# One pass of Strassen products with a second level in five of seven, operands kept in DRAM

## The chip, the cores and the metric

The kernel runs on one core of one Trainium2 chip. The metric is the time of one execution in device microseconds (us), the median of several. A profiled execution is about 1.7 us shorter, because its span runs only from the first to the last instruction. A verdict is a ratio: the mean time of one kernel's fast runs over that of the other's of the same rounds, with a 95% interval; it is called "same" where the two lie within 2%, so a "same" can still be a small difference clear of noise. So it is not quite the ratio of the medians quoted. Engine names: PE is TensorE, DVE is VectorE, ACT is ScalarE, POOL is GpSimd, SP issues DMA.

## The reference, cut to what matters

A linear attention block, then a gated MLP, each behind a layer norm and with a residual. Only the MLP matters here:

```python
x = A_x                                            # 2048 tokens x 1024
h = x + attention(layernorm(x))
g, u = layernorm(h) @ W_gate, layernorm(h) @ W_up  # 1024 x 3584 each
h2 = h + (relu(g) * u) @ W_down                    # 3584 x 1024: the down projection
```

## The kernel before

Every large product is one level of Strassen's method in Winograd's form: operands in 2 x 2 blocks, seven block products in place of eight, and sums of blocks as operands. Outputs collect in three PSUM accumulators, A, D and E, which are added to ("drained") as soon as they are complete. The gate and up products run in *chunks*, one per 128 pairs of hidden columns and token half `s`: seven products of eight matmuls each, for gate and up.

```python
def finish_sum(ps, m, q):                 # drain D or E, then relu(gate) * up
    gu = mwork.tile([P, 2, SW], BF16, tag="gu", name="gu")
    nc.vector.tensor_tensor(out=gu[:], in0=ps[:], in1=m[:], op=ALU.add)
    d = dst(q)
    nc.scalar.activation(out=gu[:, 0, :], in_=gu[:, 0, :], func=ACT.Relu)
    nc.vector.tensor_tensor(out=d, in0=gu[:, 0, :], in1=gu[:, 1, :], op=ALU.mult)
    spill(q, d)
# ... cut: part1 (products 1, 2), snap (ACT copies A) ...
def part2():
    A = st["A"]
    prod(A, 6, False)
    st["u2"] = snap(A)
    st["E"] = E = ps2.tile([P, 2, SW], FP32, tag="E", name="E")   # one buffer only
    prod(E, 5, True)
    prod(A, 7, False)
    finish_sum(E, snap(A), 3)
def part3():
    A, E = st["A"], st["E"]
    prod(A, 4, False)
    # ... cut: relu on ACT, one multiply on DVE, spill(2, d) ...
    prod(E, 3, False)
    finish_sum(E, st["u2"], 1)
```

Per chunk the code issues `part1()`, `part3()` of the chunk before, `part2()`. So E is filled by product 3 of the old chunk, must be drained by DVE, and is wanted again by product 5 of the new chunk, with only product 6 (1.73 us) in between.

The down projection runs `down(s)` once for each of two token halves. It holds all its operands on the chip and uses matmuls of 512 columns:

```python
for s in range(NS):
    down(s)      # seven products of 56 matmuls; sums of hidden blocks and of W_down made here on DVE
```

## Time and profile before

| | before |
|---|---|
| time, median (first three runs) | 769.52 us |
| span of the profile | 768.0 us |
| PE, DVE, ACT busy | 96%, 63%, 42% |
| MLP: first wide chunk to down projection | 297.81 to 594.06, 296.25 us |
| down projection, first to last matmul | 594.06 to 764.16, 170.10 us |
| tail after the last matmul | 3.84 us |

From the page: busy time by engine, and the busy share of PE and DVE in 40 equal slices, in tenths.

```profile
PE 740.3 (96%) x3584; PEld 340.2 (44%) x3584; DVE 482.0 (63%) x868; ACT 321.6 (42%) x593; POOL 6.1 (1%) x44
...
PE   5999999999889999999999999999998999999998
...
DVE  5997654886896766656474564746545991349632
```

PE is at eight or nine tenths from the second slice on; DVE has room. The chain of work that ended last shows start, duration and what it was:

```profile
592.69 1.24 DVE gu L615
...
594.06 12.25 PE accA L759 x56
606.31 12.09 PE accD L759 x56
...
752.08 12.10 PE accA L759 x56
```

One product of 56 matmuls takes 12.09 us, 216 ns each, and the products stand end to end. Next, busy times by stretch. The first number after the window is its length; then come PE, weight loads, DVE, ACT, POOL (each with its number of instructions), the granted clock (the share of its full clock that PE was given), the DMA share and GB/s.

```profile
297.81:594.06 296.25, 292.79 (x1346) 131.33 (x1344) 164.56 (x273) 125.58 (x169) 0.00 (x0) 1.00 0.23 67
594.06:764.20 170.14, 169.53 (x784) 76.60 (x784) 98.36 (x89) 0.58 (x1) 0.00 (x0) 1.00 0.52 173
```

DMA averages 173 GB/s in the down stage. Last, the timeline around the drain of E in a chunk (start, duration, instruction, and in brackets how long its engine was idle and what ended it). `E<-hs,wg` and `E<-hs,wu` are product 3, `A<-hs,..` product 6, `E<-hs,tg` product 5:

```profile
459.70 1.03 PE L596 MATMUL E<-hs,wu 128*128 128x512 f16 x4
459.77 0.69 DVE L671 TENSOR_TENSOR hh<-A,rg 128x512 bf16<-128x512 f32 x1
...
460.76 1.23 DVE L615 TENSOR_TENSOR gu<-E,snap 128x1024 bf16<-128x1024 f32 x1 [0.30 <-PE E L596]
...
461.43 1.03 PE L596 MATMUL A<-hs,tu 128*128 128x512 f16 x4
...
462.29 1.03 PE L596 MATMUL E<-hs,tg 128*128 128x512 f16 x4
```

Product 3 ends near 460.6, the drain runs from 460.76 to 461.99, and product 5 starts on time at 462.29. That is 0.3 us of slack. Where DVE makes weight sums at the same moment the slack is gone, and chunks take 12.31 or 12.45 us in place of 12.09.

### The profile page before, as it was taken

To read this page: it belongs to the slowest core of one execution; us is meant where nothing else is said; L and a number is where in the kernel's file an instruction comes from. 1 tells how busy PE (TensorE), PEld (TensorE's weight loads), DVE (VectorE), ACT (ScalarE), POOL (GpSimd) and SP (SyncE) were. 2 spreads that over 40 slices of the span, in tenths; PEclk is the share of its full clock that TensorE was granted. 3 is DMA by queue.
4 is the path that set the end of the run, shared out by engine and by line. 5 is a ranking of instruction groups with operands and counts; after the bars stand their busy time and mean duration, and the time that the engine had idled before them with its cause. 6 is when DMAs were issued, how large, how long until landed. Compare 5 with 4: busy or idle time off the path is not lost.

```text
span 768.0 us, 9610 instructions
## 1 busy us (share of the span) xinstructions
PE 740.3 (96%) x3584; PEld 340.2 (44%) x3584; DVE 482.0 (63%) x868; ACT 321.6 (42%) x593; POOL 6.1 (1%) x44
## 2 busy tenths in 40 slices
PE   5999999999889999999999999999998999999998
PEld 2444555444344444444444444444443444444443
DVE  5997654886896766656474564746545991349632
ACT  4775553877777554444444344444434000000000
POOL 0000000000000000000000000000000000000000
PEclk9999999999999999999999999999999999999999
DMA  9675003089767526154032140130001986971001
GB/s 321 145 138 150 1 1 110 1 186 225 180 154 192 121 63 209 45 152 131 7 87 72 34 131 8 55 103 29 28 7 60 331 261 209 316 256 49 28 27 55
DMA packets 125151, 89.76 MB, mean 117 GB/s; under 512 B 50352, under 2 KB 116912, under 8 KB 124592
## 3 DMA queue, kind: packets, MB, share of 16 engines
q1 hardware_dynamic: 125104, 89.15, 40.9%
q8 instruction: 28, 0.46, 0.2%
q14 instruction: 19, 0.16, 0.1%
HBM read 59.77 MB, written 17.83 MB: 101 GB/s over the span
## 4 chain that ended last, share of the span: by engine, by line
PE 64%; DVE 20%; ACT 8%; DMA 4%; issue 3%; SPq 0%; POOL 0%; DVEq 0%; ACTq 0%
PE A L596 16%; PE accA L759 11%; PE E L596 8%; PE accE L759 6%; PE attn L514 4%; DVE gu L615 4%; PE Aq L280 3%; PE Dp L596 3%; PE Aq L414 2%; PE Eq L280 2%; ACT snap L610 2%; PE Aq L629 2%; PE accD L759 2%; DVE stats L249 2%; DMA hn<-hn 1%
## 5 line engine op out<-in xcount | busy, mean ns | idle before, releaser
L615 DVE TENSOR_TENSOR gu<-E,snap 128x1024 bf16<-128x1024 f32 x48 | 58.7, 1223 | 90.1 <-ACT snap L610 87.5
L610 ACT COPY snap<-A 128x1024 f32<-128x1024 f32 x72 | 72.0, 1008 | 84.1 <-PE A L596 84.1
L759 PEld LDWEIGHTS <-hh 128*128 128x128 bf16 (+1 forms) x560 | 54.7, 98 | 67.7 <-issue 1.9
L617 ACT ACTIVATE gu<-gu 128x512 bf16<-128x512 bf16 x72 | 45.4, 630 | 86.2 <-DVE gu L615 85.9
L759 PE MATMUL accA<-wd,hh 128*128 128x512 f16 (+1 forms) x336 | 73.3, 379 | 1.4 <-DVE gu L615 1.4
L514 PE MATMUL attn<-wo_mem,oT 128*128 128x512 bf16 x256 | 59.3, 385 | 3.4 <-DVE o_sb L494 3.1
L596 PEld LDWEIGHTS <-tg 128*128 128x128 f16 x384 | 37.5, 98 | 49.5 <-issue 5.7
L596 PEld LDWEIGHTS <-tu 128*128 128x128 f16 x384 | 37.6, 98 | 45.3
L618 DVE TENSOR_TENSOR hh<-gu 128x512 bf16<-128x512 bf16 x72 | 30.5, 423 | 38.4 <-ACT gu L617 38.4
L147 ACT COPY u<-Aq 128x512 f32<-128x512 f32 x56 | 32.2, 581 | 44.5 <-PE Aq L280 20.9
L596 PE MATMUL A<-hn,tg 128*128 128x512 f16 (+1 forms) x192 | 49.3, 379 | 1.1 <-ACT snap L610 1.1
L596 PE MATMUL A<-hn,tu 128*128 128x512 f16 (+1 forms) x192 | 49.3, 379 | 0.0
L596 PEld LDWEIGHTS <-wg 128*128 128x128 bf16 x288 | 28.2, 98 | 34.5 <-issue 1.1
L596 PEld LDWEIGHTS <-wu 128*128 128x128 bf16 x288 | 28.2, 98 | 34.0
L514 PEld LDWEIGHTS <-oT 128*128 128x128 bf16 x256 | 25.2, 99 | 36.0 <-issue 8.6
L759 PEld LDWEIGHTS <-s 128*128 128x128 f16 x224 | 21.9, 98 | 27.2 <-issue 0.8
L615 DVE TENSOR_TENSOR gu<-Dp,snap 128x1024 bf16<-128x1024 f32 x24 | 29.3, 1220 | 2.3 <-PE Dp L596 2.3
L280 PEld LDWEIGHTS <-xT 128*128 128x128 bf16 (+1 forms) x192 | 18.6, 98 | 23.9 <-issue 2.4
L767 DVE TENSOR_TENSOR u<-accA,hres 128x512 f32<-128x512 f32 x16 | 10.8, 690 | 28.6 <-PE accA L759 28.1
L494 DVE TENSOR_TENSOR o_sb<-nd,rd 128x384 bf16<-128x384 f32 (+1 forms) x48 | 22.9, 508 | 8.6 <-ACT rd L493 8.3
L516 DVE SCALAR_TENSOR_TENSOR x_res<-attn,x_res 128x512 bf16<-128x512 f32 x32 | 22.0, 688 | 7.7 <-PE attn L514 7.6
L596 PE MATMUL E<-hs,tg 128*128 128x512 f16 x96 | 24.6, 378 | 0.9
(161 smaller groups left out, 1217.5 us busy)
## 6 DMA issues: line engine op xcount, KB each, us to landing
wd<-in_B_W_down_dram SPq DMA_DIRECT2D x16, 896.0 KB, 6.5
hh_dram<-hh SPq DMA_DIRECT2D x72, 128.0 KB, 1.7
wg<-in_B_W_gate_dram SPq DMA_DIRECT2D x14, 512.0 KB, 4.9
wu<-in_B_W_up_dram SPq DMA_DIRECT2D x14, 512.0 KB, 4.9
hh<-hh_dram SPq DMA_DIRECT2D x4, 1792.0 KB, 8.0
x_sb<-in_A_x_dram SPq DMA_DIRECT2D x16, 256.0 KB, 3.8
x_res<-in_A_x_dram SPq DMA_DIRECT2D x16, 256.0 KB, 3.0
h_dram<-x_res SPq DMA_DIRECT2D x16, 256.0 KB, 2.6
```

Of the source, the lines that this page charges most:

```text
L147: nc.scalar.copy(out=snaps[nm, v], in_=A[v][:])
L249: nc.vector.bn_stats(out=stats[:, k, :], in_=x_sb[:, k * NW:(k + 1) * NW])
L280: nc.tensor.matmul(ps[:], lhsT=left[m - 1][:, kc, r + v * P:r + (v + 1) * P], rhs=right[m - 1][:, kc, :], start=(start and kc == 0), stop= ...
L494: nc.vector.tensor_tensor(out=ov[:, c0:c0 + n], in0=ndv[:, :, 0:P].rearrange("p k (h e) -> p k h e", h=HPC), in1=rd[:, 0:n, :].unsqueeze(3 ...
L514: nc.tensor.matmul(ps[:], lhsT=st["oT"][:, c, :], rhs=wo_sb[:, c, j * NW:(j + 1) * NW], start=(c == 0), stop=(c == KC - 1))
L516: nc.vector.scalar_tensor_tensor(out=h_sb[:, j * NW:(j + 1) * NW], in0=ps[:], scalar=1.0, in1=h_sb[:, j * NW:(j + 1) * NW], op0=ALU.mult, ...
L596: nc.tensor.matmul(ps[:, v, :], lhsT=w[v][m - 1][:, kc, :], rhs=left[m - 1][:, kc, :], start=(start and kc == 0), stop=(kc == KH - 1), ski ...
L610: nc.scalar.copy(out=m[:], in_=ps[:])
L615: nc.vector.tensor_tensor(out=gu[:], in0=ps[:], in1=m[:], op=ALU.add)
L617: nc.scalar.activation(out=gu[:, 0, :], in_=gu[:, 0, :], func=ACT.Relu)
L618: nc.vector.tensor_tensor(out=d, in0=gu[:, 0, :], in1=gu[:, 1, :], op=ALU.mult)
L759: nc.tensor.matmul(accs[tt][:], lhsT=lhs[:, half * FD + f, tt * P:(tt + 1) * P], rhs=rhs[half][:, f, :], start=(start and half == 0 and f ...
```

## The change

The intent is to remove PE time. Both token halves go through one pass of seven outer products, and five of them get an inner Strassen level: 7 x 28 matmuls of 256 columns in place of 112 of 512. The operands are then too many for the chip. So the sums S1 to S4 of hidden blocks are made during the MLP, chunk by chunk, and go to DRAM. Sums of W_down, and of the four chunks computed early, are made there too, as "filler" between chunks. The down stage reads everything back, two products ahead.

```diff
+    def hh_sums_a(hq, s, f):
+        ...
+        nc.vector.tensor_tensor(out=s1, in0=hq[:, H21, :], in1=hq[:, H22, :], op=ALU.add)
+        nc.vector.tensor_tensor(out=s2, in0=s1, in1=h11, op=ALU.subtract)
+        nc.vector.tensor_tensor(out=s3, in0=h11, in1=hq[:, H21, :], op=ALU.subtract)
+        nc.sync.dma_start(out=x_dram[s][k][:, H22:S3 + 1, r, :], in_=hq[:, H22:S3 + 1, :])
         def spill(q, ap):
-            if s != 0 or fc < NE:
-                nc.sync.dma_start(out=hh_dram[s][q][:, fc, :], in_=ap)
+            if is_early:
+                nc.sync.dma_start(out=raw_dram[q][:, fc, :], in_=ap)
+            elif q == 2:
+                hh_sums_a(hq, s, fc)      # three sums: in part3, ahead of product 3's drain
+            elif q == 1:
+                hh_sums_b(hq, s, fc)      # the fourth
...
+    fill = [lambda f=f: early_sums(f) for f in range(NE)] + [lambda c=c: wd_sums(c) for c in range(FH // 2)]
...
             p2()
+            if k > 4 and fill:
+                fill.pop(0)()
...
-    for s in range(NS):
-        down(s)
+    OUTER = (1, 2, 6, 5, 7, 3, 4)
+    INNER = (2, 6, 5, 3, 4)
+    def inner(op, base, sink):
+        ...
+        def part1():
+            st["A"] = acc("A")
+            mm(st["A"], 1, True)              # 28 matmuls of 256 columns
+            m1 = snap(0, 0)                   # drain A on DVE
+            d = acc("D")
+            mm(d, 2, True)
+            sink(0, ALL, cols(0), view(d), m1)
+        def part2(): ...                      # 6 -> A, snap, 5 -> E, 7 -> A, snap, sink E
+        def part3(): ...                      # 4 -> A, sink, 3 -> E, sink
```

## The prediction

> **Bound now.** TensorE. The page: PE 740.3 of 768.0 us, granted clock 0.998; DVE 63%. In the chain of work that ended last the down projection runs from 594.06 to 764.2 us almost as one row of matmuls, 12.09 us per outer product of 56 (216 ns each); the busy times by stretch give 169.5 us of PE in 170.1. The gated MLP before it (297.8 to 594) is tight: 12.09 us per chunk of 56, gaps of 0.2 to 0.4 us beside DVE's weight sums.
>
> **Removed.** Both token halves go through one pass of seven outer products of 24.2 us. Five get an inner Strassen level: 7 x 28 = 196 matmuls of 256 columns in place of 112 of 512. At the column rate (108 ns) each takes 21.2 us, so 5 x 3.02 = 15.1 us of PE go: 169.3 becomes 154.2. Can 256 columns hide a weight load? The Trainium skill ("TensorE: Matmul & The Clock Gate", Back-to-back issue gap) gives 262 cycles for 256 columns in isolation, but 81 ns per load-and-matmul pair at 128. The trace disagrees with the latter: 32 matmuls of 132 columns in the kv step take 1.87 us, 58 ns each. I expect 107 to 110 ns.
>
> **Added.**
> 1. MLP: four 512-wide operand sums per chunk (0.34 us as spaced in the timeline), 1.4 us on DVE's 6.6 of 12.09, for 24 chunks; in 11 also early sums (1.4 us) or sums of W_down (about 2.4 us, estimated from 2.0 us per 3584 elements). DVE is then busy 8 to 11 us. PE's tight spot is accumulator E: DVE must drain it (1.22 us) within one product (1.73 us), 0.3 us of slack is left, and three sums now stand just before that drain. I expect 0.3 us lost per chunk, 0.5 more where filler runs: 4 to 14 us.
> 2. Down, DVE: per inner product 11.6 us of sums for the next (four of 1.94, four of 0.97), seven drains of 1024 fp32 (1.22), up to four residual adds (0.6): 20 to 22.5 us against PE's 21.2. Products 2, 6, 7 and 3 are about balanced; A and E have 1.7 us of slack. I expect 4 to 10 us of waits.
> 3. Down, DMA: operands reread, about 22 MB of x, 12 of weights, 8 of residual and output: 42 MB in some 145 us, 290 to 300 GB/s. The old stage's first half shows 283 GB/s at a DMA share of 0.85, 348 at most. 0 to 8 us of waits.
> 4. Tail: about +1 us.
>
> **Critical path.** All 15.1 us lie on it, but so do the new waits: about 8 in the MLP, 7 from DVE below, 1 or 2 from DMA and tail. Net near zero; ordering may hide more: 766 us, 80% range 754 to 784. Faster needs the whole gain.
>
> **What would show it.** Matmuls of 256 columns spaced 108 ns, PE busy near 154 us in the down stage, DVE 115 to 125; the MLP stretch 4 to 14 us over its 296, its PE idle put down to the E drain; DMA at 280 to 310 GB/s; PE waiting longer on DVE than on DMA.
>
> **What would make it wrong.** 256 columns slower than 110 ns; DMA holding back operand loads, so that DVE and then PE stand still (tens of us); DVE's narrower sums losing their rate; or DVE's order leaving the drains undelayed, which would give nearly the whole 15 us.

## The result

| | before | after |
|---|---|---|
| time, median of 4 | 769.04 us | 769.18 us |
| ratio | | 1.0002 [0.9985, 1.0019] |
| MLP stretch | 296.25 us | 303.67 us |
| down stage | 170.10 us | 159.78 us |
| tail | 3.84 us | 5.72 us |
| start of the wide chunks | 297.81 us | 298.23 us |

0.42 + 7.42 - 10.32 + 1.88 = -0.60 us, the difference of the two spans (768.0 and 767.4 us). The gain is there, and it is given back. (The profile of before has 3.4 us at half clock near 206 us, in no stage compared here; its start can be late by up to 1.7 us for it, an estimate.) The page of the kernel after:

```profile
PE 728.2 (95%) x4004; PEld 380.7 (50%) x4004; DVE 557.8 (73%) x1019; ACT 327.0 (43%) x597; POOL 6.1 (1%) x44
...
PE   5999999999889999999999999999999999999996
...
DVE  5997654786896767799797575675756359967994
```

PE lost 12 us of busy time and DVE gained 76. Busy times by stretch, columns as above:

```profile
298.23:601.90 303.67, 294.67 (x1345) 131.17 (x1344) 216.32 (x407) 126.85 (x168) 0.00 (x0) 1.00 0.49 156
601.90:761.68 159.78, 156.46 (x1205) 117.65 (x1203) 120.40 (x103) 4.68 (x5) 0.00 (x0) 1.00 0.76 268
```

In the MLP the matmuls are the same, but the stretch is 7.4 us longer and DVE is busy 216 us in place of 165. In the down stage DVE is at 120 of 160 us and DMA at 268 GB/s. PE's timeline there shows the price of a small matmul:

```profile
668.62 3.22 PE L919 MATMUL accD<-w,x 128*128 128x256 f16 x28
671.67 3.22 PE L919 MATMUL accA<-ws,x 128*128 128x256 f16 x28
674.73 1.47 PE L919 MATMUL accE<-w,xs 128*128 128x256 f16 x12
```

28 matmuls of 256 columns take 3.06 us from start to start, 109.2 ns each. Five products of 196 and two of 112 at 216 ns make 155.4 us (107.0 + 48.4), so 4.4 of the 159.78 us are waits. The drain of E in a chunk, to be set against the one shown of before:

```profile
515.77 1.03 PE L638 MATMUL E<-hs,wu 128*128 128x512 f16 x4
515.85 0.69 DVE L723 TENSOR_TENSOR hq<-A,rg 128x512 bf16<-128x512 f32 x1
...
516.58 0.43 DVE L606 TENSOR_TENSOR hq<-hq 128x512 f16<-128x512 bf16 x1
...
516.92 0.42 DVE L608 TENSOR_TENSOR hq<-x,hq 128x512 f16<-128x512 bf16 x1
517.26 0.42 DVE L607 TENSOR_TENSOR hq<-hq,x 128x512 f16<-128x512 f16 x1
...
517.59 1.22 DVE L667 TENSOR_TENSOR gu<-E,snap 128x1024 bf16<-128x1024 f32 x1
...
518.86 0.81 PE L638 MATMUL E<-hs,tg 128*128 128x512 f16 x3
```

The three operand sums (L606, L608, L607) stand between the multiply and the drain (L667). Product 3 ends near 516.6; the drain starts at 517.59, about 0.8 us later than it did before, and product 5 starts as the drain ends, at 518.86. Over the last thirteen chunks the mean is 12.45 us for 12.22.

Now the first waits of the down stage. This is the chain of work there:

```profile
611.97 14.21 DMA x<-x_dram
626.19 2.04 DVE xs L867
...
632.13 2.02 DVE xs L872
634.15 1.14 DVE snap L925
...
640.21 3.23 PE accA L919 x28
```

A load of an operand lands after 14.2 us, DVE makes its sums, then drains A, and PE follows.

### The profile page after: what moved, and what is told of

It is laid out like the page before. It is cut to its first block, busy times and chain, and to the rows that moved or that the text cites. A ratio compares the mean times of both kernels' runs of the same rounds, so it can differ in the third digit from the quotient of the medians.

```text
span 767.4 us, 10597 instructions
## 1 busy us (share of the span) xinstructions
PE 728.2 (95%) x4004; PEld 380.7 (50%) x4004; DVE 557.8 (73%) x1019; ACT 327.0 (43%) x597; POOL 6.1 (1%) x44
## 4 chain that ended last, share of the span: by engine, by line
PE 26%; DVE 21%; DMA 5%; ACT 4%; issue 3%; SPq 2%; DVEq 0%; ACTq 0%
PE A L638 7%; DVE gu L667 6%; PE accA L919 6%; PE E L638 4%; PE accE L919 3%; DVE hq L723 2%; DMA x<-x_dram 2%; DMA hq<-raw_dram 2%; ACT gu L669 2%; ACT snap L662 2%; PE accA L963 2%; PE Dp L638 1%; DMA wraw<-in_B_W_down_dram 1%; PE accD L919 1%; DVE hq L606 1%
## 5 line engine op out<-in xcount | busy, mean ns | idle before, releaser
L667 DVE TENSOR_TENSOR gu<-E,snap 128x1024 bf16<-128x1024 f32 x48 | 58.6, 1220 | 48.0 <-ACT snap L662 48.0
L919 PEld LDWEIGHTS <-x 128*128 128x128 f16 (+1 forms) x560 | 54.8, 98 | 9.1 <-issue 2.2
L919 PEld LDWEIGHTS <-xs 128*128 128x128 f16 x420 | 41.1, 98 | 7.0 <-issue 2.2
L670 DVE TENSOR_TENSOR hq<-gu 128x512 bf16<-128x512 bf16 x48 | 20.2, 421 | 22.5 <-ACT gu L669 22.5
L963 PEld LDWEIGHTS <-x 128*128 128x128 bf16 (+1 forms) x224 | 21.9, 98 | 26.0
L919 PE MATMUL accA<-w,x 128*128 128x256 f16 (+1 forms) x280 | 32.2, 273 | 0.3 <-DVE snap L925 0.2
L667 DVE TENSOR_TENSOR gu<-Dp,snap 128x1024 bf16<-128x1024 f32 x24 | 29.3, 1220 | 1.3 <-PE Dp L638 1.3
L638 PE MATMUL A<-hn,wg 128*128 128x512 bf16 x96 | 27.1, 379 | 2.0 <-DVE hq L723 2.0
```

What stands on the lines that cost most here:

```text
L638: nc.tensor.matmul(ps[:, v, :], lhsT=w[v][m - 1][:, kc, :], rhs=left[m - 1][:, kc, :], start=(start and kc == 0), stop=(kc == KH - 1), ski ...
L919: nc.tensor.matmul(pv[:, tt, :], lhsT=op["left"][m - 1][:, f, tt * P:(tt + 1) * P], rhs=op["right"][m - 1][:, f, :], start=(start and f == ...
L963: nc.tensor.matmul(pss[p][:, t * NW:(t + 1) * NW], lhsT=op["x"][s][kh][:, f, (t0 + t) * P:(t0 + t + 1) * P], rhs=op["w"][kh][:, f, :], sta ...
```

## The experiments

Theory A: the MLP's loss is a matter of DVE's *order*, sums ahead of the drain of E. Rivals: B, the added DMA traffic; C, DVE's *load*, wherever the sums stand. For the filler a theory D was added: DVE stands in its queue before a load that has not landed. For the down stage the rivals are DMA and DVE's order.

One caution holds for all: the comparison with the reference called no_hh, no_wd and own_x correct although their operands are wrong. The MLP's share of the output is too small for it to notice. "Correct" below therefore rests on the edit as well.

**Stretches of every profiled run** (us; "ten" is the interval from the first to the eleventh chunk, where the filler of after runs; "later" is the mean of the thirteen intervals after that):

| run | ten | later | down | tail |
|---|---|---|---|---|
| before | 119.0 | 12.22 | 170.1 | 3.8 |
| after | 124.0 | 12.45 | 159.8 | 5.7 |
| no_hh | 128.4 | 12.27 | 162.0 | 5.2 |
| no_wd | 127.0 | 12.45 | 160.4 | 5.2 |
| after_drain | 123.4 | 12.36 | 160.1 | 5.7 |
| all_plain | 122.8 | 12.45 | 169.4 | 5.6 |
| held | 126.4 | 12.22 | 164.0 | 5.7 |
| prefetch | 123.5 | 12.47 | 160.2 | 5.8 |
| end | 125.1 | 12.45 | 160.6 | 5.3 |
| own_x | 122.9 | 12.45 | 162.0 | 5.9 |
| prefetch2 | 132.5 | 12.45 | 161.4 | 5.4 |
| no_loads | 122.4 | 12.45 | 161.8 | 5.7 |
| best2 | 126.1 | 12.09 | 161.9 | 5.0 |
| final2 | 117.4 | 12.09 | 162.7 | 5.5 |

"Later" falls into clear steps. "Ten" and "down" scatter by some us between kernels in which that part was not edited. One reason is in the clock records: in some profiles the granted clock falls to 0.50 for 3.4 us, and matmuls of 512 columns then follow each other every 427 ns and not 216. Each such stretch costs about 1.7 us (worked out from these figures, so an estimate). There is one in the ten chunks of no_wd, held and best2, two in a row (6.8 us) in those of prefetch2, and one in the down stage of held; the ten and down intervals of the other runs have none. Each came during or just after waits of PE of 2 us or more, but such waits also passed without one (no_hh), and what starts them was not tested.

### no_hh: the operand sums out of the MLP

```diff
-        nc.vector.tensor_tensor(out=s1, ...)   # and s2, s3, s4
+        nc.gpsimd.memset(hq[:, S1:S3 + 1, :], 0.0); nc.gpsimd.memset(hq[:, S4, :], 0.0)   # in new_hq
```

> Wrong result on purpose: the operand sums of the hidden tensor (four VectorE operations per chunk, the early chunks' too) are not computed; GpSimd writes zeros in their place, and every transfer stays. In the kernel after, the gated MLP takes 303.7 us from its first wide chunk to the down projection against 296.3 before, and its later chunks 12.45 us on average against 12.23. Theory A (VectorE's order: sums stand before the drain of accumulator E): the later chunks return to 12.2 us and the stretch to 297 to 299 us; total about 763 to 765. Rival B (the added DMA traffic of these stores and reloads costs the time): nothing changes, 769.

Measured: 772.52 us, ratio 1.0049. The total went the wrong way, but the parts tell more. The later chunks fell from 12.45 to 12.27 us, with every transfer still there, so B is out for them. The first ten rose to 128.4 us, because DVE now stood still for the filler's loads (from the list of waits: engine, line, waited for, us in total, times, longest):

```profile
DVE wt L594 <- DMA wraw<-in_B_W_down_dram: 17.4, 5, 6.9
```

That is where theory D came from.

### no_wd: the W_down sums out of the filler

```diff
-        nc.vector.tensor_tensor(out=t[:, 0], ...)   # and t[:, 1], t[:, 2], t[:, 3]
+        nc.gpsimd.memset(t[:], 0.0)
```

> Wrong result on purpose: the four VectorE sums of W_down per filler piece are replaced by one GpSimd fill; their loads and stores stay. Theory A (VectorE's time in the filler chunks): the first ten chunks, now 124.0 us against 119.0 before, lose about 2 us; total about 767. Rival B (DMA: the 7.3 MB of W_down read and 3.7 MB stored during those chunks): nothing changes, 769.

Measured: 770.40 us, ratio 1.0014; ten chunks 127.0 us. Taking DVE's work away gained nothing in all. One wait weighs most:

```profile
PE E L635 <- DVE gu L664: 5.6, 1, 5.6
...
DVE hq L603 <- DMA hq<-raw_dram: 5.3, 1, 5.3
```

A sum of an early chunk stood 5.3 us in DVE's queue for its load, the drain of E stood behind it, and PE lost 5.6 us. A stretch at half clock followed (359.6 to 363.0 us), for about 1.7 us more. Without these two the ten chunks would have taken 119.7 us, 4.3 less than in after (an estimate). So the run shows what one late load can cost; it does not show that DVE's time in the filler costs nothing. It is not clean either: the GpSimd fill also waited for stores of its buffer, which moved the transfers about.

### after_drain: the sums issued behind the drain

```diff
-            elif q == 2:
-                hh_sums_a(hq, s, fc)
             elif q == 1:
+                hh_sums_a(hq, s, fc)
                 hh_sums_b(hq, s, fc)
```

> Correct result: the three operand sums that stood before the drain of accumulator E are issued behind it, together with the fourth. The same work, the same transfers. Theory A (it is the place of the sums, not their amount): the later chunks fall from 12.45 to about 12.25 us, total about 764 to 766. Rival C (it is VectorE's load, 66% to 85% in the MLP, wherever the sums stand): 769, with the wait moved to another accumulator.

Measured: 767.42 us, ratio 0.9983 [0.9970, 0.9997]; later chunks 12.36 us, half of what A expected. The timeline says why:

```profile
526.92 0.69 DVE L722 TENSOR_TENSOR hq<-A,rg 128x512 bf16<-128x512 f32 x1
...
527.64 0.42 DVE L606 TENSOR_TENSOR hq<-hq 128x512 f16<-128x512 bf16 x1
527.99 0.42 DVE L608 TENSOR_TENSOR hq<-x,hq 128x512 f16<-128x512 bf16 x1
...
528.32 1.22 DVE L666 TENSOR_TENSOR gu<-E,snap 128x1024 bf16<-128x1024 f32 x1
...
529.45 0.42 DVE L607 TENSOR_TENSOR hq<-hq,x 128x512 f16<-128x512 f16 x1
```

Two of the three sums still run ahead of the drain (528.32). So the order in DVE's queue, settled by the build, is not the order in the source.

### held: an order edge behind the drain

```diff
-            nc.vector.tensor_tensor(out=gu[:], in0=ps[:], in1=m[:], op=ALU.add)
+            drain = nc.vector.tensor_tensor(out=gu[:], in0=ps[:], in1=m[:], op=ALU.add)
...
-            spill(q, d)
+            with tc.issue_after(drain.ins):     # queued behind the drain on DVE; waits for nothing
+                spill(q, d)
```

(together with after_drain's edit)

> Correct result. In after_drain only one of the three sums really moved: the order in which instructions are queued is settled when the kernel is built, and two sums still stood before the drain of accumulator E. Here an order edge on VectorE puts all four sums behind that drain. Theory A (their place costs the time): the later chunks, 12.45 us in after and 12.36 in after_drain, come to 12.25 us, total 764 to 766. Rival C (VectorE's load): no better than after_drain, 767.4, or worse.

Measured: 765.56 us (764.02 to 770.04), ratio 0.9950 [0.9929, 0.9971]; later chunks 12.22 us, exactly before's.

```profile
527.00 0.69 DVE L723 TENSOR_TENSOR hq<-A,rg 128x512 bf16<-128x512 f32 x1
...
527.80 1.23 DVE L666 TENSOR_TENSOR gu<-E,snap 128x1024 bf16<-128x1024 f32 x1
...
528.95 0.41 DVE L606 TENSOR_TENSOR hq<-hq 128x512 f16<-128x512 bf16 x1
...
529.28 0.42 DVE L608 TENSOR_TENSOR hq<-x,hq 128x512 f16<-128x512 bf16 x1
...
529.61 0.42 DVE L607 TENSOR_TENSOR hq<-hq,x 128x512 f16<-128x512 f16 x1
```

The drain follows the multiply at once and the sums come after it. The same DVE work and the same transfers no longer cost anything in the later chunks: A holds there, B and C fall. The profiled run was the slowest of the six. Its 126.4 us in the first ten chunks and 164.0 in the down stage each hold one stretch at half clock (at 380.9 and 729.1 us), so about 1.7 us of each is the clock's.

### prefetch and prefetch2: the filler's loads ahead of time

```diff
-            if k > 4 and fill:
-                fill.pop(0)()
+            if k > 3 and fill:
+                ld, fn, c = fill.pop(0); loaded.append((fn, c, ld(c)))    # load one piece ahead
+            if k > 4 and loaded and (len(loaded) > 1 or not fill):
+                fn, c, v = loaded.pop(0); fn(c, v)                        # sums of the piece before
```

The W_down pieces are halved so that two fit.

> Correct result. The filler (sums of the early chunks and of W_down) has its loads issued one piece ahead and the W_down pieces halved, so that the same VectorE work no longer stands in its queue waiting for a load just issued. Theory D (the filler costs by such waits: VectorE idles 7.2 us before filler operations for DMA in after, 19 us in no_hh which lost the most there): the first ten chunks go from 124.0 to about 121.5 us, the waits on DMA vanish, total 766 to 767. Rival A' (the filler costs by VectorE's time, or by DMA bandwidth): no change, 769.

Measured: 769.01 us, ratio 0.9991; ten chunks 123.5 us. The waits moved: DVE now waited 4.3 us for stores of its own sums and 3.3 us for loads. The second try issued the loads from GpSimd (`nc.gpsimd.dma_start`) and made the W_down sums in place, with three buffers.

> Correct result. prefetch was no clean test: VectorE then waited on the stores of the W_down sums (4.3 us) and on loads queued late behind other transfers (3.3 us). Here the filler's loads go out from GpSimd's own queue, one piece ahead, and the W_down sums are made in place, with three buffers. Theory D (the filler costs by VectorE standing in its queue before an operand that has not landed): VectorE's waits on DMA in the filler fall below 2 us, the first ten chunks go from 124.0 to about 121.5 us, total 766 to 767. If GpSimd's queue brings its own cost, or if it is VectorE's time, no change or worse, 769 or more.

Measured: 779.21 us, ratio 1.0126; ten chunks 132.5 us, of them about 3.4 the clock's, with DVE's waits on DMA still at 8 us. Both failed as tests of D: the waits they were to remove did not go, and each changed where the build put the filler. The Trainium skill ("DMA: Bandwidth & Descriptors", Issuing engines are not separate DMA queues) says that another issuing engine saves only the issuing time, as all run on the same 16 DMA engines. No run here tests that alone, as prefetch2 changed buffers and order too.

### all_plain: the inner level undone

```diff
-    INNER = (2, 6, 5, 3, 4)
+    INNER = ()
+    flat = {1: sink1, 7: sink7, 2: onto_out(0, 0, u2), 6: onto_u(u2, u2), 5: onto_u(u5, u2),
+            3: onto_out(0, 1, u5), 4: onto_out(1, 0, u2)}
```

> Correct result: the inner Strassen level is undone in all five products (112 matmuls of 512 columns each), all else as after: one pass, sums in the MLP, operands from DRAM. If the inner level is worth its matmuls less its waits (PE 169.3 for 155.4 us, less 4.4 us of waits), the down stage goes from 159.8 to about 169.5 us and the total to about 779. If the waits of the down stage come from DMA and not from the inner level, they stay and the total is about 783.

Measured: 776.77 us, ratio 1.0108 [1.0090, 1.0126].

```profile
599.93:769.31 169.38, 169.38 (x785) 76.56 (x783) 45.61 (x48) 4.68 (x5) 0.00 (x0) 1.00 0.72 254
```

PE is busy for all of the 169.38 us. The operands still come from DRAM, at 254 GB/s, and hold nothing up. So the 4.4 us of waits in after belong to the inner level, and its worth in the profile is 169.4 - 159.8 = 9.6 us of the 13.9 that its matmuls save. (The medians of the whole, 776.77 and 769.18 us, differ by 7.6; 779 was expected.)

### own_x and no_loads: less DMA in the down stage

```diff
-        if k == 1:
+        if k in (1, 2):           # own_x: the second product reuses the operand on the chip
             op["xt"] = x1
+        if n >= 3:                # no_loads: tiles of the product two before, nothing loaded
+            old = ops[n - 2]; op = {"k": k, "wt": old["wt"], "xt": old["xt"]}; ...; return op
```

> Wrong result on purpose: the second outer product reads the operand that is already on the chip in place of the one loaded from DRAM (3.7 MB less in the first 25 us of the down stage). Theory: the first two waits of the down stage (about 1.4 us of PE at 635 to 640 us) begin with that load, which lands at 626 us at over 300 GB/s and holds back VectorE's sums; without it they vanish and the total is about 768. Rival: VectorE's order alone makes them, and they stay, 769.

> Wrong result on purpose: from the fourth outer product on nothing is loaded in the down stage; each product takes the operand tiles of the one two before it. PE and VectorE do the same work in the same buffers. In after the down stage takes 159.8 us for 155.4 of matmuls. If DMA landing late makes the waits after the second product (in held 6 us of waits, three of them begun by loads), they shrink and the stage falls to 158 to 159 us, total about 768; if VectorE's order alone makes them, nothing changes. If DMA were the limit of the whole stage, it would fall further, but it cannot fall below 156 to 157.

Measured: own_x 771.94 us (ratio 1.0026 [1.0003, 1.0048], where about 768 us was expected), no_loads 770.33 us (1.0009, result wrong). The down stage took 162.0 and 161.8 us for 159.8. In no_loads DMA ran at 128 GB/s:

```profile
602.34:764.09 161.75, 156.68 (x1203) 117.65 (x1203) 121.01 (x103) 4.68 (x5) 0.00 (x0) 1.00 0.37 128
```

Taking the loads away did not take the waits away, so DMA is not what limits this stage as a whole. Single waits can still begin with a load, and own_x speaks for it. In after the first two waits of the stage, near 635 and 640 us, cost PE 1.4 us; the chain above begins them with a load. In own_x, without that load, 0.2 us is left of them. But others came, 1.2 and 1.9 us for drains of A at 665 and 670 us, where after had 0.2 us. The build had ordered DVE's queue anew, and the waits of the stage came to 6.6 us for 4.4.

### end: the last product rearranged

```diff
+            if last:
+                dd()              # product 2 into D, now behind product 7, to cover the drain of A
...
-            sink(0, ALL, cols(1), view(st["E"]), st["u2"])
+            for ts in ((slice(0, 2), slice(2, 4)) if last else (ALL,)):
+                sink(0, ts, cols(1), view(st["E"])[:, ts, :], st["u2"][:, ts, :])
```

> Correct result. In the last inner product the product into D is moved behind the seventh, so that it fills the time in which VectorE drains A for the fourth (PE waits 1.3 to 1.5 us there now), and the last drain is split by token halves with two smaller stores. Expected: that wait falls below 0.3 us, the tail after the last matmul from 5.7 to about 4.5 us, total 766.5 to 767. If the tail is set by the store's own landing time and not by its size, only 1.3 us are gained.

Measured: 770.41 us, ratio 1.0009: no gain. PE's waits at the end, in after and in end:

```profile
755.40 3.22 PE L919 MATMUL accA<-ws,x 128*128 128x256 f16 x28 [1.31 <-DVE snap L925]
```

```profile
737.77 3.22 PE L919 MATMUL accA<-ws,x 128*128 128x256 f16 x28 [1.67 <-DVE snap L925]
```

The wait of 1.31 us went, and one of 1.67 us appeared 18 us earlier: the product into D had been covering the drain of the outer product before. The tail was 5.3 us for 5.7.

### best2 and final2: the order settled

best2 puts together held, prefetch2 and end, makes the gate and up weight sums one unit ahead (the last two lines of the diff below), and in the second outer product queues four operand sums behind the first drain of A (`with tc.issue_after(snaps[-1].ins): some(4)`), so that the drain comes first.

> Correct result. Four edits that leave the arithmetic as it is: operand sums behind the drain of E by an order edge (held), filler loads ahead from GpSimd's queue (prefetch2), the gate and up weight sums prepared one unit ahead and also behind that drain, the end rearranged (end), and in the second product the drain of A queued before its last four sums. If the waits found so far are the whole loss: later chunks 12.1 us (12.22 in before), MLP stretch about 294 to 297 us, down stage 157 to 158, total 755 to 760. If they only move, 764 to 767.

Measured: 770.67 us, ratio 1.0018. The later chunks took 12.09 us, the rate of the matmuls, but the first ten took 126.1 with prefetch2's filler. The last run dropped prefetch2's filler, end's rearrangement and best2's edge behind the drain of A, and placed the original filler:

```diff
+            if k > 4 and k % 2 and fill:               # every second chunk, before p2()
+                with tc.issue_after(drains[-1].ins):   # DVE's part behind the latest drain of E
+                    fill.pop(0)()
+            if (s, f, wt_, fi) == items[0] and units:  # gate and up weight sums, one unit ahead
+                with tc.issue_after(drains[-1].ins): prepare(units.pop(0))
```

With held's edit, and the drains of the last outer product split by token halves (`for ts in (slice(0, 2), slice(2, 4))`).

> Correct result. The arithmetic of after, with VectorE's order settled by edges: in every chunk of the MLP the three accumulator drains come first and the operand sums, the weight sums (prepared one unit ahead) and the filler follow the drain of E; the filler is spread over every second chunk, so that its loads have two chunks to land, and goes out from the ordinary queue; in the last inner product the drains are split by token halves. If VectorE's order is what ate the gain of the inner level: chunks of 12.1 us throughout, MLP stretch 290 to 293 us (296 in before, 304 in after), down stage 159 to 161, total 756 to 761, faster than both by 1 to 1.7%. If the filler still costs its 3 to 5 us however placed: 762 to 764.

Measured: 758.49 us (757.32 to 759.54), before 768.89; ratio 0.9848 [0.9829, 0.9867], so 1.5% faster than before.

```profile
300.00:345.00 45.00, 45.00 (x211) 20.37 (x209) 33.07 (x69) 19.19 (x26) 0.00 (x0) 1.00 0.45 134
345.00:390.00 45.00, 45.00 (x210) 20.43 (x209) 34.58 (x67) 19.86 (x27) 0.00 (x0) 1.00 0.47 145
390.00:424.00 34.00, 34.00 (x160) 15.36 (x158) 23.69 (x43) 14.08 (x20) 0.00 (x0) 1.00 0.61 186
```

PE is busy for every microsecond of the windows that hold the start of the filler (the sums of the early chunks); in after it was busy 43.16, 42.61 and 33.38 us of the same three. The sums of W_down follow between 437 and 585 us and cost nothing either: every chunk takes 12.09 us, and the MLP stretch is 291.34 us (298.15 to 589.49). The expected 159 to 161 us of down stage did not come: it took 162.7, and 6 us of its waits are for drains of A. Where in that order the loss lies stays open.

The 1.5% is not the worth of the inner level alone. Of the 10.2 us between the two profiles (768.0 and 757.8), 4.9 lie in the MLP (296.25 to 291.34), where before had gaps of its own beside its weight sums. Before with its weight sums put behind the drain of E was not run; it might win much of these 4.9 us without the change.

## Why the prediction was right, point by point

1. **The gain.** 15.1 us of PE time were forecast, at 108 ns per matmul. At 109.2 ns, 13.9 us were saved (169.3 - 155.4). The case against the pairwise figure of the skill, read from the kv step, was right.
2. **The MLP.** 4 to 14 us were forecast, "about 8"; it was 7.4. The named cause, sums before the drain of E, is shown by held, for the later chunks. Its size was 0.23 us per chunk, not 0.3.
3. **The filler.** "0.5 more where filler runs", some 5.5 us in all, was too much, and its reason, DVE's added time, was incomplete. After 0.23 for each of the ten intervals, 2.7 of their 5.0 us are left for it (worked out, so an estimate). DVE's time alone does not cost it: final2 does the whole filler at no loss. In no_wd and no_hh the largest waits are DVE standing before late loads. How much of the 2.7 us in after comes from such loads, and how much from sums that stand ahead of a drain, no run tells apart; in final2 placing and spacing were changed together.
4. **The down stage.** 4 to 10 us of waits on DVE were forecast, 4.4 came. DVE was busy 120 us (115 to 125 forecast). In the list of PE's waits in that stage DVE is named alone (2.8 us for drains of A, 0.4 us for one of E), and DMA never; yet by the chain above and by own_x the first two of these waits began with a load on which DVE waited. DMA averaged 268 GB/s, under the 280 to 310 forecast.
5. **The tail.** +1 forecast, +1.9 measured: the last drain is twice as wide and an add follows it. DVE's part after the last matmul grew from 0.69 to 1.91 us; the other 0.7 was not taken apart.
6. **The middle.** The terms of the text add to about +1 us, yet the middle was set at 766 us, 3 below before, because "ordering may hide more". The opposite held: the order was the loss, and the time came out at 769.18. That the sum of the terms was so close is in part luck: 1.2 us less were saved and the tail cost 0.9 more, while the waits below were 4.4 us for some 7 and the filler cost about half of what was allowed for it.

## What to carry to other kernels

When an engine that is not the bottleneck gets more work, ask first what will stand ahead of the operation that the bottleneck waits for, and only then how busy the engine becomes: here 50 us more of DVE work cost 7 us in one order and nothing in another. The order in the queue need not be the order in the source, so read it from the trace and pin it where there are only tenths of a microsecond of slack. And an operation whose load is issued just ahead of it can hold up everything behind it in its queue: queue the operation behind the urgent work, as final2 did. Issuing the load earlier was tried twice here (prefetch, prefetch2) and did not pay.

## What the Trainium skill lacked or had wrong

- "TensorE: Matmul & The Clock Gate", Back-to-back issue gap: its table gives 262 cycles for 256 columns, which is 109 ns at 2.4 GHz; the runs show 109.2 ns with a weight load for each matmul. Its sustained figures do not fit: 131 ns for 512 columns against 216 ns here, and 81 ns for 128 against 58 ns for 132 columns (32 in 1.87 us, from before):

```profile
109.08 2.04 PE L349 MATMUL kv_ps<-v_sb,wo_mem 128*128 128x132 bf16 x32
110.95 0.81 PE L280 MATMUL Aq<-wv_sb,xT 128*128 128x512 bf16 x3
```

- "TensorE: Matmul & The Clock Gate" (specification table) has VectorE's queue as strictly first in, first out. The trace agrees (no_wd: a drain stood 5.3 us behind a sum that waited for its load). What the pages I read lack is the consequence: that occupancy says little about such a queue. DVE at 71% in the MLP of after (216 of 304 us) held PE up; at 75% in final2 (219 of 291 us) it did not.
- "DMA: Bandwidth & Descriptors" (Specifications) gives a limit of about 358 GB/s of HBM per core without a condition. The same page, under its measured bandwidths, says that it is for both cores of a pair streaming. One slice of the profile page of after shows 401 GB/s over 19 us for a kernel on one core, which agrees with that note; the row of the table lacks it.
